# Loads, layer-norm roots, dummy matmuls and the job order of a one-core transformer kernel

## The chip, the core and the metric

The kernel runs on one core of a Trainium2 chip. The core has five engines that run their own instruction streams: PE (TensorE, matrix products, and transposes as products with an identity), DVE (VectorE), ACT (ScalarE), POOL (GpSimd) and SP (SyncE, here a queue that issues DMAs). They wait for each other on semaphores; each executes its own stream in order. Products accumulate in PSUM, which has 8 banks of 512 f32 columns; SBUF holds the rest. The metric is device time in microseconds of one execution, median of the runs.

## The reference

A layer norm of x (2048 tokens, width 448) feeds two branches, and the output is their sum with x:

```python
x = A_x
xn = _layernorm(x, axis=-1)
return x + _A_ref(xn, A_wqkv, A_w_phi, A_wo) + _B_ref(xn, B_w1, B_w2, B_w3, B_w4)

# A: 16 heads of 28; q, k, v from xn @ wqkv
pq = einsum("bhsd,hdf->bhsf", q, w_phi)          # the same for k
phi_q = concat([softmax(pq), softmax(-pq)])      # the same for k
kv = einsum("bhsf,bhsd->bhfd", phi_k, v);  z = einsum("bhsf->bhf", phi_k)
o = einsum("bhqf,bhfd->bhqd", phi_q, kv) / (einsum("bhqf,bhf->bhq", phi_q, z) + 1e-6)
A = o @ wo

# B: a mixer with four quarters of h shifted by 1, -1, 2, -2 tokens, then an MLP of width 1792
h = gelu(layernorm(xn) @ w1)
x1 = xn + shift(h) @ w2
B = x1 + gelu(layernorm(x1) @ w3) @ w4
```

## The kernel before

All inputs are bf16. The tokens are 16 tiles of 128 (t0 to t15), in 4 groups of 512. The width of 448 is split into 4 chunks of which PE works on row halves: a matmul uses either the lower or the upper 64 rows of the array, and one of each runs at a time. A product therefore has a list of lower and a list of upper matmuls, and writes its bank first from one half, then from the other.

A small recording layer (`Recorder`) takes the operations in the order in which the program text makes them, works out which semaphores each must wait for, and plays them to the engines. So the order of the text is the order of every engine's stream, of the two queues of DMAs (SP's, and ACT's, whose issues stand among ACT's work) and of PE above all.

The head (up to about 38 us in the profile):
- Loads: x tiles by `load_x`, wv and w1 by `load_half` in two halves (256 rows each, overlapping by 64), on SP and ACT by turns (L367 to L379). Then wphi, and `load_wT`: the q and k blocks of wqkv, transposed by DMA (t=1 for k, t=0 for q). `load_w2`, `load_w4` and `load_lap(w3)` come later, all on SP.
- Layer norm of a tile: "m" statistics and aggregate on DVE, "r" the power -0.5 on POOL (`ln_scale`), "a" the apply on DVE, or "p" the apply on POOL after a negated mean (`ln_neg`). The sums of tile 1 are made on ACT instead (`ln1_sums`).
- `XT`: the normalised tile transposed on PE into two banks (`xn_T`) and moved to `xnT` by ACT or DVE (`xn_out`); `XD`: the same by a DMA.
- `ZV(i)`: v of tile i into bank vb[i], moved by ACT or DVE (`EV`). `ZW(g, m)`: 128 columns of w1 for a group of 512 tokens into bank gb[g][m], gelu by ACT (`EW`). `ZR`: the last 64 columns of w1. `FO`: w_phi folded into a q or k block (`fold`), evicted by DVE. `rest_T` and `h_shift` are DMAs that bring h in place for w2.
- `HF`: halves of the first pair's products with the folded k and q and with w2.
- `spin` writes dummy matmuls on a constant to keep PE going; `busy`, their operand, is a piece of gT that DVE fills.

`chain` takes these jobs and lays the lower matmuls of a job out at once, its upper ones after a lag of 600 columns, between the lower ones of later jobs.

The rest is one list, played in order. For a pair n of tiles: (k0,n),(k1,n) and (q0,n),(q1,n) are first and second halves of the products, each followed by two Exp on ACT; (w0,i),(w1_,i) the w2 product and its sum into xn on DVE; kn and kx normalise phi_k (DVE, POOL); K is kv of a tile; T, G transposes by DMA; lo, sc, A the second layer norm; (a,p),(b,p) first and second half of a w3 product of 256 columns, followed by a gelu; N the attention output of a tile; (f,1..4,k) four parts of the last product for two tiles; S the store. The pair's banks are `kq[n]` and `wb[i]` (pair b means banks 2b and 2b+1).

Of the kernel before, what the change touches and what calls it, by code (L numbers as in the profile page):

```python
# [224 lines left out]
def bass_parallel_sum__linear_kernel_hedgehog__mixer_s_mlp__prompt_kernel(  # L225
# [17 lines left out]
    with es:  # L243
# [50 lines left out]
        wo = wv  # L294
# [116 lines left out]
        busy = gT[:, 0, 0, 0:256]  # L411
        R.ew(dve, "memset", busy, 1.0)
# [78 lines left out]
        def spin(n, cols):  # L491
            for _ in range(n):
                R.mm(banks[7][:, 0:cols], busy[:, 0:128], busy[:, 0:cols], True, True)
# [393 lines left out]
        def ln1(*ops):  # L887
            for op, *n in ops:
# [11 lines left out]
        fb = {(1, 0): 2, (1, 2): 2, (0, 0): 2, (0, 2): 5}  # L900
# [34 lines left out]
        kq = {0: (2, 0), 1: (1, 3), 2: (0, 1), 3: (0, 2), 4: (1, 2), 5: (1, 2), 6: (1, 2), 7: (1, 0)}  # L935
        wb = {0: 3, 2: 2, 4: 2, 6: 0, 8: 0, 10: 0, 12: 2, 14: 2}
# [3 lines left out]
        def HF(p, n):  # L940
# [4 lines left out]
        vb = {0: 7, 1: 6, 2: 0, 3: 2, 4: 4, 5: 5, 6: 1, 7: 0, 8: 4, 9: 5, 10: 0, 11: 6, 12: 3, 13: 2, 14: 0, 15: 1}  # L945
        gb = ((5, 2, 3), (7, 6, 5), (4, 1, 0), (7, 7, 4))
        spin(39, 128)
        ln1_sums(1)
        chain([
            L(("m", 0), ("m", 2), ("r", 0, 1), ("a", 0), ("m", 3), ("v", 1), ("r", 1, 2), ("a", 2), ("a", 1), ("r", 3, 1)),  # L950
            XT(0, 2, 1, "ACT"), do(spin, 5, 256), L(("a", 3), ("m", 4), ("m", 5), ("r", 4, 1), ("r", 5, 1)),
            inside(1, ZV(0, EV(0, "ACT", 1)), XT(2, 5, 1, "ACT")), XT(3, 3, 1, "ACT"), ZV(2, EV(2, "ACT", 1)),
            inside(1, ZV(3, EV(3, "ACT", 1)), XT(1, 3, 1, "ACT")), ZV(1, EV(1, "ACT", 1)), L(("a", 4), ("m", 7)),
            ZW(0, 0, EW(0, 0, 1)), L(("a", 5)), XT(5, 0, 1, "ACT"),
            L(("m", 6), ("m", 9), ("r", 7, 1), ("m", 8), ("r", 6, 1), ("r", 8, 1), ("a", 7), ("a", 6), ("m", 10)), ZW(0, 2),
            L(("m", 11), ("a", 8)), XD(8), L(("m", 12)), XT(4, 0, 1, "ACT"), L(("r", 9, 1)), ZW(0, 1, EW(0, 1, 2)), L(("a", 9)),
            ZV(4, EV(4, "ACT", 1)), XD(9), XT(7, 0, 1, "ACT"), L(("r", 10, 2), ("a", 10)), XT(6, 6, 1, "ACT"), L(("m", 13)),
            ZV(5, EV(5, "ACT", 1)), do(phi_blocks), ZV(7, EV(7, "DVE", 1)), ZW(1, 1, EW(1, 1, 1)), ZV(6, EV(6, "ACT", 1)),
            L(("p", 11), ("r", 12, 1), ("m", 15)), inside(2, ZW(1, 0, EW(1, 0, 1)), XT(10, 2, 1, "ACT")), L(("r", 13, 1)),
            ZW(1, 2, EW(1, 2, 1)), L(("p", 12), ("r", 15, 1)), inside(3, ZV(8, EV(8, "ACT", 1)), FO(1, 0, 0)), L(("m", 14)),  # L960
            XD(11), L(("r", 14, 1)), do(load_wT, 0, (1, 2, 3)), L(("a", 13)), inside(1, ZV(10, EV(10, "ACT", 1)), FO(1, 0, 1)),
            L(("a", 15)), ZR(0, 7, (rest_out, 0, 7), (rest_T, 0), (h_shift, 0)), ZV(9, EV(9, "DVE", 1)), XT(12, 3, 1, "ACT"),
            L(("p", 14)), do(load_w2), XT(13, 1, 1, "ACT"), ZV(11, EV(11, "ACT", 1)), ZW(2, 2, EW(2, 2, 1)), do(late_3),
            XT(14, 2, 2, "DVE"), ZW(2, 0, EW(2, 0, 1)), ZW(2, 1, EW(2, 1, 1)), do(load_lap, w3, B_w3), FO(1, 2, 0),
            inside(3, ZW(3, 0, EW(3, 0, 1)), FO(1, 2, 1)), ZR(1, 6, (rest_out, 1, 6)),
            inside(3, ZW(3, 2, EW(3, 2, 1)), FO(0, 0, 0)), ZV(15, EV(15, "ACT", 1)), do(kv_ones),
            inside(3, ZW(3, 1, EW(3, 1, 1)), FO(0, 0, 1)), do(rest_T, 1), inside(1, ZV(14, EV(14, "ACT", 1)), FO(0, 2, 0)),
            FO(0, 2, 1), ZV(13, EV(13, "ACT", 1)), ZV(12, EV(12, "DVE", 1)), HF(0, 0), do(kv_picks), HF(1, 0), HF(2, 0), HF(0, 1),
            do(h_shift, 1), HF(1, 1), do(load_w4), HF(2, 1)], 600, 1)

        on_dve = (4, 6, 7, 9, 12)
# [58 lines left out]
        def wo_in():  # L1030
            load_lap(wo, A_wo)
# [3 lines left out]
            (T, 0), (T, 1), (k0, 1), (w0, 2), (kn, 0), (k1, 1), (w1_, 2), (lo, 0), (q0, 1), (k0, 2), (kx, 0), (k1, 2), (kn, 1), (w0, 4),  # L1035
            (kx, 1), (q1, 1), (T, 2), (T, 3), (q0, 2), (lo, 1), (w1_, 4), (kn, 2), (q1, 2), (T, 4), (T, 5), (lo, 3), (k0, 3), (K, 0), (k1, 3), (kn, 3),
            (kx, 2), (lo, 2), (kx, 3), (q0, 3), (sc, 0), (K, 1), (q1, 3), (T, 6), (T, 7), (A, 1), (A, 0), (k0, 4), (G, 0), (A, 3), (w0, 6),
            (A, 2), (K, 2), (k1, 4), (G, 1), (G, 2), (K, 3), (G, 3), (q0, 4), (w1_, 6), (q1, 4), (k0, 5), (K, 4), (kn, 4),
            (w0, 8), (k1, 5), (q0, 5), (kx, 4), (K, 5), (lo, 4), (w1_, 8), (kn, 5), (q1, 5), (K, 6), (k0, 6), (w0, 10),
# [49 lines left out]
```

## Time and profile before

| | us |
|---|---|
| median of 3 runs (173.91 to 174.32) | 173.97 |
| the profiled execution | 174.06 |
| its span, first to last instruction | 172.3 |

The granted clock of TensorE is 1.00 in every stretch of the span. By stretch, busy time in us of each engine (and its instructions), as the profile's windows give it:

| stretch, us | what runs | PE | DVE | ACT | POOL |
|---|---|---|---|---|---|
| 0 to 7.57 | loads, dummies, first tiles' layer norm | 5.12 (x53) | 3.93 (x13) | 3.51 (x7) | 4.22 (x23) |
| 7.57 to 15 | v, w1, layer norm | 7.20 (x109) | 7.19 (x21) | 5.46 (x11) | 3.54 (x6) |
| 15 to 33 | v, w1, folds | 17.96 (x359) | 11.66 (x30) | 13.40 (x24) | 9.03 (x15) |
| 33 to 46 | first pairs | 12.90 (x135) | 9.69 (x17) | 10.56 (x13) | 3.87 (x2) |
| 46 to 80 | k, q, w2, kv, first w3 | 33.97 (x564) | 29.29 (x45) | 26.05 (x31) | 28.12 (x16) |
| 80 to 88 | w3, first attention tiles | 7.91 (x104) | 7.27 (x21) | 3.35 (x5) | 3.69 (x5) |
| 88 to 165 | w3, w4, attention out | 77.00 (x958) | 40.43 (x107) | 19.68 (x20) | 36.90 (x56) |
| 165 to 172.3 | last tiles, stores | 4.84 (x44) | 1.41 (x3) | 0.00 (x0) | 0.65 (x1) |

Busy time of PE is the union of pipelined matmuls, so a stretch can look full while single matmuls start late. ACT loads a function table three times: at 0.80 (gelu), 34.18 (Exp) and 67.41 (gelu), 1.28 each. The first transfers, from issue to landing: x0 and x1 2.4 and 2.6, x2 and x3 2.6 and 2.8, the wv halves 4.8 (SP) and 5.7 (ACT), x4 and x5 5.4 and 5.8, the w1 halves 6.2 and 6.5; a half of w3 4.8 and 6.5, w4 10.0.

### The profile page before, as it was taken

What the parts mean: (1) busy time and instruction counts of PE and PEld (TensorE: products, weight loads), DVE (VectorE), ACT (ScalarE), POOL (GpSimd) and SP (SyncE); (2) the same over time, 40 slices, a digit from 0 to 9 for tenths busy, and PEclk for the clock granted to TensorE, in tenths of its full rate; (3) what the DMA queues carried; (4) which work ended last, traced back from release to release, by engine and by line L of the source; (5) the groups of instructions that cost most, each with busy time, mean ns of one, the idle gap of its engine ahead of it and who ended that gap; (6) DMA issues with size and microseconds to landing.
All of it is one profiled execution on the core that took longest, in us unless ns stands there. A gap on an engine that the chain in (4) does not pass through costs nothing.

```text
span 172.3 us, 5315 instructions
## 1 busy us (share of the span) xinstructions
PE 166.9 (97%) x2308; PEld 96.6 (56%) x2308; DVE 110.9 (64%) x251; ACT 82.0 (48%) x107; POOL 90.0 (52%) x121
## 2 busy tenths in 40 slices
PE   7799999999999999999999999999999999999994
PEld 7545888874555555554544554554545545555563
DVE  3799943749999989918955873525817416474621
ACT  4478876777987899646133322133133212044000
POOL 5456970004779999860574289332441522724540
PEclk9999999999999999999999999999999999999999
DMA  5995546499998955161057557554961120233331
GB/s 127 330 248 92 104 67 158 87 352 220 334 159 174 135 124 138 21 76 30 11 114 97 111 105 146 94 103 106 136 135 34 30 57 4 57 34 84 88 87 50
DMA packets 51111, 20.07 MB, mean 116 GB/s; under 512 B 42256, under 2 KB 50384, under 8 KB 51088
## 3 DMA queue, kind: packets, MB, share of 16 engines
q1 hardware_dynamic: 49968, 18.86, 56.0%
q10 hardware_dynamic: 1120, 0.87, 1.6%
q8 instruction: 18, 0.29, 0.8%
q14 instruction: 5, 0.04, 0.1%
HBM read 7.14 MB, written 1.84 MB: 52 GB/s over the span
## 4 chain that ended last, share of the span: by engine, by line
PE 92%; DMA 3%; ACT 1%; DVE 1%; issue 0%; ACTq 0%
PE banks L204 91%; DMA wv<-in_A_wqkv_dram 3%; PE banks L208 1%; ACT xnT L212 1%; DVE wpq L216 1%; ACT vaug L212 0%; ACTq L222 0%; ACT L366 0%; DVE vaug L216 0%
## 5 line engine op out<-in xcount | busy, mean ns | idle before, releaser
L212 ACT ACTIVATE phik<-banks 128x1024 bf16<-128x1024 f32 (+1 forms) x44 | 42.2, 986 | 63.6 <-PE banks L204 63.4
L204 PE MATMUL banks<-gT,w 64*128 64x512 bf16 x392 | 49.2, 376 | 0.1
L216 DVE TENSOR_TENSOR vaug<-banks,vaug 128x464 f32<-128x464 f32 (+3 forms) x65 | 32.8, 513 | 20.6 <-PE banks L204 18.9
L204 PE MATMUL banks<-w,phik 64*128 64x448 bf16 (+3 forms) x434 | 45.2, 343 | 0.0
L216 POOL TENSOR_TENSOR xnT<-vaug 128x196 bf16<-128x196 f32 (+1 forms) x32 | 18.1, 587 | 47.8 <-DVE vaug L216 47.8
L204 PE MATMUL banks<-wv,xnT 64*128 64x448 bf16 (+3 forms) x222 | 32.8, 346 | 1.4 <-DMA wv<-in_A_wqkv_dram 1.2
L204 PEld LDWEIGHTS banks<-w,phik 64*128 64x128 bf16 (+1 forms) x434 | 22.9, 94 | 19.4 <-issue 0.4
L722 POOL TENSOR_TENSOR phik<-phik,rks 128x1792 bf16<-128x1792 bf16 x8 | 25.6, 3214 | 10.7 <-DVE rks L216 10.5
L204 PEld LDWEIGHTS banks<-gT,w 64*128 64x128 bf16 x392 | 18.0, 94 | 18.7 <-PE banks L204 1.1
L204 PEld LDWEIGHTS banks<-wv,xnT 64*128 64x128 bf16 (+1 forms) x222 | 13.8, 94 | 10.0 <-ACT xnT L212 1.6
L216 POOL TENSOR_TENSOR vaug<-xn,xtok 128x448 f32<-128x448 bf16 x16 | 16.2, 1033 | 0.2 <-DVE vaug L216 0.2
L216 DVE TENSOR_REDUCE ksum<-phik 128x64 f32<-128x1792 bf16 x8 | 16.0, 1994 | 0.0
L216 POOL TENSOR_TENSOR rs<-mv,mhalf 128x1 f32<-128x1 f32 (+2 forms) x18 | 12.4, 694 | 6.6 <-DVE mv L216 6.6
L204 PE MATMUL banks<-xnT,w 64*128 64x512 bf16 x84 | 15.7, 377 | 0.0
L216 DVE RECIPROCAL vaug<-banks 128x16 f32<-128x16 f32 x16 | 4.0, 252 | 17.4 <-PE banks L204 17.4
L204 PE MATMUL banks<-wpk,xnT 64*128 64x448 bf16 x112 | 14.9, 350 | 0.1
L212 ACT ACTIVATE hi<-banks 128x896 bf16<-128x896 f32 x16 | 13.8, 931 | 1.0 <-PE banks L204 1.0
L204 PE MATMUL banks<-wpq,xnT 64*128 64x448 bf16 x112 | 14.2, 349 | 0.0
L204 PE MATMUL banks<-w,hT 64*128 64x448 bf16 x96 | 12.9, 349 | 0.0
L216 DVE TENSOR_TENSOR xn<-banks,xn 128x512 bf16<-128x512 f32 (+1 forms) x16 | 9.0, 606 | 3.0 <-PE banks L204 2.9
L216 DVE BATCH_NORM_STATS2 st<-xn 128x6 f32<-128x448 bf16 x16 | 9.4, 589 | 0.0
L216 DVE BATCH_NORM_STATS2 st<-xtok 128x6 f32<-128x448 bf16 x15 | 9.1, 606 | 0.0
(72 smaller groups left out, 165.4 us busy)
## 6 DMA issues: line engine op xcount, KB each, us to landing
w<-in_B_w_dram SPq DMA_DIRECT2D x2, 896.0 KB, 5.7
out_dram<-vaug SPq DMA_DIRECT2D x15, 112.0 KB, 2.0
w<-in_B_w_dram SPq DMA_DIRECT2D x1, 1568.0 KB, 10.0
xtok<-in_A_x_dram SPq DMA_DIRECT2D x2, 448.0 KB, 7.4
wv<-in_A_wo_dram SPq DMA_DIRECT2D x2, 224.0 KB, 2.9
xtok<-in_A_x_dram SPq DMA_DIRECT2D x3, 112.0 KB, 2.6
xtok<-in_A_x_dram ACTq DMA_DIRECT2D x3, 112.0 KB, 2.8
w<-in_B_w_dram SPq DMA_DIRECT2D x1, 336.0 KB, 4.3
```

The costliest lines, as they stand in the source:

```text
L204: self.op("PE", lambda e: e.matmul(out, lhsT, rhs, start=start, stop=stop, skip_group_check=True), [out], [lhsT, rhs], tile=self._tile(lhsT))
L208: self.op("PE", lambda e: e.transpose(out, in_, ident), [out], [in_, ident], tile=self._tile(in_))
L212: self.op("ACT", lambda e: e.activation(out, in_, func, **kw), [out], [in_] + aps)
L216: self.op(eng, lambda e: getattr(e, name)(out, *args, **kw), [out], aps)
L722: R.op(pool, lambda e: e.tensor_tensor(ph, ph, wide, op=ALU.mult), [ph], [ph, wide, *after])
```

## The change

- wv's halves are issued right after x0 and x1, ahead of x2 and x3; half 0 of wv and of w1 is now SP's, half 1 ACT's.
- The roots of tiles 1 to 7 are made on ACT ("q", `ln_root`), whose preloaded table is now that of the reciprocal root; a table load before the first gelu is added by that.
- Tiles 2, 3, 4, 5, 7, 12, 14, 9, 10, 11 are applied on POOL (before: 11, 12, 14), the others on DVE. Tiles 9 to 12 go through DMA transposes (before: 8, 9, 11).
- The first group of w1 is made in halves of 256 tokens (`ZH`), three products of two halves each. `z_h`, which nothing called, is removed.
- The dummies read a constant tensor; besides `spin`, `HD` puts short groups of half-height dummies between the first tiles.
- w2 is loaded on ACT's queue, w3 in two halves at two places (the second behind w4 and the h shifts), wo on ACT's queue.
- Banks vb, gb, fb, kq, wb are given anew, and both lists are in another order.

```diff
-        R.op("ACT", lambda e: e.preload_act_table_set("gelu_apprx_tanh_and_others"), [], [])
+        R.op("ACT", lambda e: e.preload_act_table_set("abs_reciprocal_sqrt_and_small"), [], [])
         load_x(0, 1)
         load_x(1, 1, "ACT")
+        load_half(wv, wv_d, 0)
+        load_half(wv, wv_d, 1, "ACT")
         load_x(2, 1)
         load_x(3, 1, "ACT")
-        load_half(wv, wv_d, 1)
-        load_half(wv, wv_d, 0, "ACT")
         load_x(4, 1)
         load_x(5, 1, "ACT")
-        load_half(w1, B_w1, 1)
-        load_half(w1, B_w1, 0, "ACT")
+        load_half(w1, B_w1, 0)
+        load_half(w1, B_w1, 1, "ACT")
...
-        busy = gT[:, 0, 0, 0:256]
-        R.ew(dve, "memset", busy, 1.0)
+        busy = nc.const_aps.tensor(1.0, [128, 128], BF16)
...
+        def ln_root(a, n):
+            R.act(rs[:, a:a + n, 0], mv[:, a:a + n, 1], ACT.Abs_reciprocal_sqrt)
...
-        def spin(n, cols):
+        def spin(n):
             for _ in range(n):
-                R.mm(banks[7][:, 0:cols], busy[:, 0:128], busy[:, 0:cols], True, True)
+                R.mm(banks[7][:, 0:128], busy, busy, True, True)
+
+        def hold(b, n):
+            return [[(banks[b + k][:, 0:128], busy[r, :], busy[r, :], True) for _ in range(n)]
+                    for k, r in enumerate((slice(0, 64), slice(64, 128)))]
...
+                if eng == "2":
+                    R.act(d[:, :, 0, :], a[:, :, 0, :], ACT.Copy)
+                    R.ew(dve, "tensor_copy", d[:, :, 1, :], a[:, :, 1, :])
...
+        def z_w1h(m, b, h):
+            c = slice(256 * h, 256 * h + 256)
+
+            def make(rows, kcs):
+                lo, hi = rows
+                return [(banks[b][:, c], w1[lo:hi, kc, 128 * m:128 * m + 128], xnT[lo:hi, kc, c],
+                         rows == LO and n == 0 and h == 0) for n, kc in enumerate(kcs)]
             return make
...
-        kq = {0: (2, 0), 1: (1, 3), 2: (0, 1), 3: (0, 2), 4: (1, 2), 5: (1, 2), 6: (1, 2), 7: (1, 0)}
-        wb = {0: 3, 2: 2, 4: 2, 6: 0, 8: 0, 10: 0, 12: 2, 14: 2}
+        kq = {0: (3, 2), 1: (3, 3), 2: (0, 1), 3: (0, 3), 4: (1, 2), 5: (1, 2), 6: (1, 2), 7: (1, 0)}
+        wb = {0: 0, 2: 1, 4: 2, 6: 0, 8: 0, 10: 0, 12: 2, 14: 2}
...
-        spin(39, 128)
+        spin(30)
         ln1_sums(1)
         chain([
-            L(("m", 0), ("m", 2), ("r", 0, 1), ("a", 0), ("m", 3), ("v", 1), ("r", 1, 2), ("a", 2), ("a", 1), ("r", 3, 1)),
-            XT(0, 2, 1, "ACT"), do(spin, 5, 256), L(("a", 3), ("m", 4), ("m", 5), ("r", 4, 1), ("r", 5, 1)),
-            inside(1, ZV(0, EV(0, "ACT", 1)), XT(2, 5, 1, "ACT")), XT(3, 3, 1, "ACT"), ZV(2, EV(2, "ACT", 1)),
...
+            do(spin, 3), L(("m", 0), ("r", 0, 1), ("a", 0), ("v", 1), ("m", 2)), L(("q", 1, 1)), do(spin, 3), HD(2, 3),
+            L(("a", 1)), HD(0, 3), L(("m", 5)), XT(0, 4, 1, "ACT"), L(("q", 2, 1)), HD(2, 3), HD(2, 3), L(("p", 2)),
+            HD(6, 2), XT(1, 2, 1, "ACT"), L(("m", 3)), ZV(0, EV(0, "ACT", 1)), L(("q", 5, 1)),
+            inside(1, ZH(2, 0), XT(2, 6, 1, "ACT")), L(("p", 5), ("m", 4), ("q", 3, 1), ("m", 6)), ZV(1, EV(1, "ACT", 1)),
+            L(("m", 7), ("q", 4, 1)), inside(1, ZV(2, EV(2, "ACT", 1)), XT(5, 6, 1, "ACT")), L(("p", 3)), L(("q", 6, 1)),
+            ZH(1, 0), XT(3, 4, 1, "2"), ZV(5, EV(5, "ACT", 1)), L(("q", 7, 1), ("a", 6), ("m", 12)), ZH(0, 0), L(("p", 4)),
+            ZH(0, 1, EW(0, 0, 1)), XT(4, 4, 1, "ACT"), XT(6, 0, 1, "DVE"), ZH(2, 1), L(("p", 7)), ZH(1, 1, EW(0, 1, 2)),
+            L(("r", 12, 1)), XT(7, 4, 1, "ACT"), L(("m", 14)), ZV(3, EV(3, "ACT", 1)), ZV(4, EV(4, "ACT", 1)),
+            ZW(1, 0, EW(1, 0, 1)), L(("p", 12)), L(("m", 15), ("r", 14, 1)), XD(12), do(load_w3, 0),
+            L(("r", 15, 1), ("p", 14), ("m", 13), ("r", 13, 1), ("m", 10), ("a", 15), ("r", 10, 1)),
+            do(load_wT, 0, (1, 2, 3)), ZW(1, 1, EW(1, 1, 1)), ZV(6, EV(6, "ACT", 1)), L(("m", 9)), XT(14, 2, 2, "DVE"),
...
         play([
-            (T, 0), (T, 1), (k0, 1), (w0, 2), (kn, 0), (k1, 1), (w1_, 2), (lo, 0), (q0, 1), (k0, 2), (kx, 0), (k1, 2), (kn, 1), (w0, 4),
...
-            (kc,), (w1_, 14), (b, 5), (kb,), (a, 6), (b, 6), (lo, 8), (N, 0), (T, 8), (a, 7), (lo, 11), (lo, 10), (f, 1, 0), (N, 1), (T, 9),
-            (b, 7), (a, 8), (sc, 8), (A, 10), (A, 8), (b, 8), (f, 2, 0), (lo, 12), (A, 9), (G, 8), (A, 11), (G, 9), (a, 9),
...
+            (w0, 2), (k0, 1), (kn, 0), (w1_, 2), (T, 0), (k1, 1), (k0, 2), (w0, 4), (kn, 1), (k1, 2), (T, 1), (q0, 1),
+            (lo, 0), (kx, 0), (q0, 2), (q1, 1), (w1_, 4), (q1, 2), (k0, 3), (q0, 3), (T, 2), (kx, 1), (k1, 3), (kn, 2),
...
+            (a, 5), (wo_in, "ACT"), (a, 6), (sc, 8), (kb,), (b, 5), (A, 9), (b, 6), (N, 0), (f, 1, 0), (N, 1), (a, 7),
+            (a, 8), (A, 8), (A, 10), (T, 11), (b, 7), (b, 8), (f, 2, 0), (lo, 13), (A, 11), (G, 10), (a, 9), (lo, 12),
...
```

## The prediction, made before the changed kernel was run

> **What bounds the kernel now.** I read the busy shares, then the chain of waits, then the timeline of PE. The shares say that PE is the bound of the whole span:
>
> ```profile
> span 172.3 us, 5315 instructions
> PE 166.9 (97%) x2308; PEld 96.6 (56%) x2308; DVE 110.9 (64%) x251; ACT 82.0 (48%) x107; POOL 90.0 (52%) x121
> ```
>
> The chain of waits (start, length, what) shows where PE is not the bound: until wv has landed, in two places of the head where ACT moves a transposed tile (10.08, 12.39), and at the last folded weight (30.18).
>
> ```profile
> 1.74 5.70 DMA wv<-in_A_wqkv_dram
> 7.43 0.14 issue
> 7.57 0.21 PE banks L204
> ...
> 10.08 0.50 ACT xnT L212
> ...
> 12.39 0.61 ACT xnT L212
> ...
> 30.18 1.10 DVE wpq L216
> ...
> 169.88 0.36 DVE vaug L216
> ```
>
> The timeline of PE gives its pace and its hidden stalls (start, length, what, count):
>
> ```profile
> 13.17 1.03 PE L204 MATMUL banks<-xnT,w 64*128 64x512 bf16 x8
> 40.33 0.92 PE L204 MATMUL banks<-wpq,xnT 64*128 64x448 bf16 x8
> 41.09 1.73 PE L204 MATMUL banks<-wpk,xnT 64*128 64x448 bf16 x14
> 78.93 1.92 PE L204 MATMUL banks<-gT,w 64*128 64x512 bf16 x14
> 84.81 2.57 PE L204 MATMUL banks<-gT,w 64*128 64x512 bf16 x20
> ```
>
> Matmuls run in pairs, one per row half. One of 512 columns lasts 0.38, so four pairs in 1.03 start (1.03-0.38)/3 = 0.217 apart; with 448 columns, (0.92-0.35)/3 = 0.190. That is 2.4 columns per ns plus 2.5 ns a matmul. By that pace the other three rows should last 6x0.19+0.35 = 1.49, 6x0.217+0.38 = 1.68 and 9x0.217+0.38 = 2.33: each is 0.24 too long. In each, the second half of a job follows the first half at once ((k0,2) and (k1,2); (a,6) and (b,6); (a,8) and (b,8)) and writes the same banks from the other row half, which waits for PE's own last writes.
>
> I gave every matmul of the order of before this pace, summed per row half and took the longer half: 159.46 us from the first wv matmul on. 7.57 + 159.46 = 167.03, but PE's last matmuls stand at 169.68. So 2.65 us after 7.57 are stalls, and only these, the start, and the work itself can change: 0.85 from 8 to 15, about 0.7 from 28 to 39, 0.7 in the three self-waits, and 0.4 in small ones.
>
> **The change, part by part.**
>
> *Work.* Twelve PE transposes of tiles instead of thirteen, the products of w1's rest in another balance of row halves, and tile 1's transposes ahead of the first wv matmul: the same sum is 159.11 for the order of after, -0.35. Halving the first w1 chunk streams the same columns (21+21 of 256 for 21 of 512). The dummies (36 full, 28 half ones) fill time in which PE has nothing; the 39 of before went 0.107 apart until 5.07, so 48 from about 0.85 end at 5.3, before tile 0 is normalised (5.37).
>
> *Start.* wv is second on both queues. Landings of before by place in the queue: SP 3.2, 3.9, then wv 1.71+4.8 = 6.5, x4 7.6, w1 8.9; ACT 3.4, 4.1, then wv 7.4, x5 8.0, w1 9.2. In both kernels 448 KB stand up to the third place, so x2 should land at 6.5 and wv before it, between the second and third place (4.1 to 7.4; I take 5.8 and 6.8). But DVE now has the statistics of x2 ahead of tile 1's apply, and PE has tile 1's transposes ahead of the first wv matmul. Statistics 6.57 (landing +0.1), aggregate 7.30, apply 7.41 to 7.82, transposes 7.87 to 8.01: the first wv matmul goes from 7.57 to 8.01, +0.44, and wv is not what it waits for. If x2 lands at 4.1 this is 6.9, but then the first w1 half (8.9) holds the third job anyway, so the gain is at most 0.3; if at 7.4, it costs 0.9 more.
>
> *Head to 18 us.* Tiles 2 to 5, 7, 12 and 14 are applied on POOL, tiles 2 to 7 with the root on ACT. Rows:
>
> ```profile
> 18.49 0.19 POOL L216 TENSOR_SCALAR rs<-mv 128x1 f32<-128x1 f32 x1
> 18.77 0.77 POOL L216 TENSOR_SCALAR xn<-xtok,rs 128x512 bf16<-128x512 bf16 x1
> ...
> 21.13 0.77 POOL L216 TENSOR_SCALAR xn<-xtok,rs 128x512 bf16<-128x512 bf16 x1
> ```
>
> So a tile on POOL costs 0.29+0.77 = 1.06 (0.41 on DVE before). A root on ACT shows nowhere; bounds are the 0.20 of the one-column ACT row at 4.21 and the 0.56 of POOL's power; I take 0.20, the same engine and shape. Walking the queues with these, 0.49 from one ACT move to the next and 0.84 for statistics and aggregate on DVE:
> - w1's first half lands 8.86, its matmul starts 8.98 where PE is free at 8.76: 0.2.
> - x5 (8.06): aggregate till 9.09, root 9.34, POOL 9.42 to 10.48; PE wants it at 10.44: 0.1. Tile 3 follows on POOL till 11.50, wanted 11.47: 0.1.
> - Tile 6's transposes need the bank of v2, which ACT empties 12.85 to 13.39 because the root of tile 7 stands ahead; wanted 13.17: 0.25.
> - A new table load before the first gelu: 15.28 to 16.56, gelus till 18.1. Tiles 14 and 15 need those banks; PE arrives at 18.05: 0.1, the rest is hidden behind five jobs whose banks are free. Without that cover it would cost 1.28.
>
> With small gaps at switches, 1.0 is lost from 8.01 to 20, where before lost 0.85 by 25.
>
> *20 to 37 us.* Tile 8's apply stands on DVE behind the eviction of a folded weight (1.09, from about 22.0), so its transposes come 0.3 late. On SP, half of w3 (896 KB) goes ahead of the three last transposed wq blocks: before, such a half took 4.8 to land and the transposes 2.9 to 3.8; issued after tile 12's transpose (17.1), they land by 24.1 to 26, and PE wants the last at about 25.1: 0 to 0.9, I take 0.2. w2's three issues on ACT (about 0.46 each, as the wv row at 1.74) end before its next gelu is needed. The first hRT transpose is queued behind six h shifts (0.6 each) and lands near 34.5, wanted at 35.5. I add 0.2 for the rest; before lost 0.7 here.
>
> *37 us to the end.* Every first and second half now has other work between. That removes the three self-waits (0.7); the other 0.4 may be replaced: I leave 0.2. I checked each w3 job against the gelu that frees its banks (1.02+0.2): the least cover is 1.40. On SP, w4 goes out some 6 us earlier (about 33 for 39.3; it took 10.0), the second h shifts and half of w3 (4.8) behind it, then the transposes of q: the first should land near 47 (50.2 before), wanted by the fifth pair's Exp at 53.6; the shifts near 44, wanted at 51. wo's issue on ACT lies in idle time (3.75 before one gelu).
>
> *Sum.* 8.01+159.11 = 167.12; +1.0+0.7+0.2 = 169.0 against 169.68: -0.7. The profiled execution took 174.06 with a span of 172.3; the median of the runs is 173.97. 173.97-0.7 = **173.3 us**.
>
> *A rule against this change.* Before, the last Exp, the load and the first gelu stand so:
>
> ```profile
> 65.66 1.73 ACT L212 ACTIVATE hi<-banks 128x896 bf16<-128x896 f32 x2
> 67.41 1.28 ACT L212 ACT_TABLE_LOAD   x1
> 68.70 1.02 ACT L212 ACTIVATE phik<-banks 128x1024 bf16<-128x1024 f32 x1
> ```
>
> The gelu starts 0.01 after the load, the load 0.02 after the Exp: a switch costs 1.3. The Trainium skill (ScalarE: Activation LUTs, "What ACT_TABLE_LOAD costs") puts 1.28 for the load and another 1.38 of drain on every switch; this trace shows no such drain.
>
> **The rivals.**
> 1. *The head runs clean* (tile and root shorter, x2 early): its 1.0 shrinks to 0.3 and the start to 7.7. 173.3-0.7-0.1 = 172.5. For: PE's waits in my walk are 0.1 each, near the error of a row. Against: tile 6 and w1 are fixed by rows.
> 2. *Nothing is left*: the re-ordered jobs make as many self-waits and bank waits as they remove, so the 0.7 of the end doesn't come: 174.0. For: six of the jobs' bank pairs changed. Against: in the written order no two halves are neighbours.
> 3. *Slower: POOL bounds the head.* From 9.4 to 18 POOL has six tiles and three powers in series, and each is fed by an ACT root behind a DVE aggregate behind x5's landing. Its tile took 0.91 at 16.57 and its power up to 0.68: six times 0.14 and three times 0.1 make tile 14 late by 1.1, of which 0.3 is slack; x5 0.5 later (its bounds are x4's 7.6 and w1's 9.2) adds 0.5. 173.3+1.3 = 174.6. It decides once tile 14 ends after 18.1, and is slower than before once it ends after 18.8. For: POOL is idle there now, DVE has slack it no longer needs. Against: two of three rows are 0.77.
> 4. *Slower: w3's half holds the wq blocks*: the last lands at 26.5, +1.2: 174.5.
> 5. *Slower: a drain behind the new table load.* If ACT stood idle after it as long as after the load at 34.18 (1.18, there put down to PE), the gelus would end at 19.3 and tiles 14 and 15 wait that long: 173.3+1.2 = 174.5. For: no load stands amid crowded ACT work in this trace. Against: the row at 68.70. The Trainium skill's page on ScalarE, above, is the rule for it; by its 1.38 the estimate would be 174.7.
>
> **How the numbers follow.** Forecast 0.45 (own range 172.8 to 173.9), rival 1 0.17, rival 2 0.13, rival 3 0.14, rival 4 0.05, rival 5 0.06. A difference under 0.3%, 0.5 us, can't be told from none: faster is below 173.45, slower above 174.5. Of the forecast's 0.45 some 0.31 lie below 173.45. Faster 0.31+0.17 = 0.48; same 0.14+0.13 = 0.27; slower 0.25. The range is 172.3 to 174.7: it takes in rivals 1 to 4 and the bounds of x2 and of the blocks.
>
> **What would show it.** The first wv matmul near 8.0, right after tile 1's transposes, with DVE's statistics of x2 ahead; an ACT table load near 15.3 and tiles 14 and 15 close behind the gelus; no wait over 0.2 on PE after 37. I am wrong if the first wv matmul starts before 7.4 or after 8.6, if PE waits for a wq block or for POOL more than 0.5, or if waits of PE on itself are still there after 40.

## The result and the profile after

| | before | after |
|---|---|---|
| median, us (6 runs each, side by side) | 174.03 (173.79 to 174.32) | 176.06 (175.60 to 177.85) |
| ratio to before, 95% interval | | 1.0127 [1.0098, 1.0157] |
| measured again beside other kernels | 174.35 (17 runs) | 177.06 (6 runs), 1.0144 [1.0091, 1.0196] |
| profiled execution and its span | 174.06, 172.3 | 176.22, 174.5 |

The change makes the kernel slower by 2.0 us. 173.3 was predicted, with a range up to 174.7. Intervals here leave executions that were disturbed out; medians and ranges are of all.

The page of the changed kernel, first its busy shares:

```profile
span 174.5 us, 5399 instructions
PE 166.2 (95%) x2341; PEld 101.4 (58%) x2341; DVE 112.4 (64%) x247; ACT 81.7 (47%) x112; POOL 92.2 (53%) x129
```

PE's busy time is 0.7 us less (166.9 before); the span has grown by 2.2, so PE waits more. The waits (in total, times, longest) say for what; PEld is PE's load of weights:

```profile
POOL phik L734 <- DVE g_tok L216: 3.3, 1, 3.3
PEld banks L204 <- POOL phik L734: 2.0, 1, 2.0
...
PE banks L204 <- DMA xnT<-xn: 1.7, 1, 1.7
PEld banks L204 <- DMA hi<-in_A_wqkv_dram: 1.2, 3, 0.4
```

Three places, none of which was on the prediction's list of PE's waits as large as this: the q blocks of wqkv (1.2), one tile that a DMA transposes (1.7), and POOL's product of phi_k (2.0). In the timeline of PE (start, length, what, count, idle time before and its releaser) they stand here:

```profile
24.05 0.21 PE L204 MATMUL banks<-g_tok,hi 48*128 48x56 bf16 x2 [0.25 <-DMA hi<-in_A_wqkv_dram]
24.54 0.21 PE L204 MATMUL banks<-g_tok,hi 48*128 48x56 bf16 x2 [0.27 <-DMA hi<-in_A_wqkv_dram]
...
27.93 0.35 PE L204 MATMUL banks<-wv,xnT 64*128 64x448 bf16 x1 [1.65 <-DMA xnT<-xn]
...
79.62 0.63 PE L204 MATMUL banks<-vaug,phik 64*128 64x59 bf16 x32 [1.90 <-POOL phik L734]
```

To see what each is worth I used the prediction's pace: the start of a matmul plus all work that is left behind it is the end that PE would reach without a further stall, its projected end. A wait costs 0.1 to 0.3 more in this end than the idle time that the timeline gives. Both kernels by time:

| near, us | before | after | after minus before |
|---|---|---|---|
| first wv matmul (7.57; 6.71) | 167.0 | 165.8 | -1.2 |
| 22 | 167.85 | 166.40 | -1.45 |
| 28 | 168.09 | 169.76 | +1.7 |
| 77 | 169.1 | 169.91 | +0.8 |
| 81 | 169.5 | 171.97 | +2.45 |
| end | 169.68 | 171.90 | +2.2 |

So the head gains 1.45 until 22 us. Between 22 and 28 this and 1.7 more is lost for two DMA waits. From 28 to 77 the kernel before loses 1.0 in its self-waits and small stalls and the changed one 0.15, so 0.9 comes back. One wait at 79.6 costs 2.05.

SP's queue around the first two (start, length, what, count):

```profile
14.21 1.26 SPq L219 DMA_TRANSPOSE xnT<-xn  x1
15.52 1.78 SPq L222 DMA_DIRECT2D w<-in_B_w_dram  x1
17.35 3.74 SPq L219 DMA_TRANSPOSE hi<-in_A_wqkv_dram  x3
21.13 5.63 SPq L219 DMA_TRANSPOSE xnT<-xn  x3
```

The second row is the half of w3 (896 KB), the third the q blocks, the fourth tiles 10, 11 and 9. w3 lands at 21.63, the q blocks at 23.54, 24.01 and 24.49, tile 10 at 27.79. On ACT's queue the three parts of w2 are issued from 21.00 on and land at 25.61, 27.53 and 28.16.

The third wait, in the timelines of DVE and POOL of the changed kernel (kn6 and kn7 are the sums of phi_k for the last two pairs, kx6 and kx7 POOL's products for them):

```profile
70.02 3.51 DVE L216 TENSOR_SCALAR g_tok<-xn,mv,rs 128x512 bf16<-128x512 bf16 x2
73.45 2.00 DVE L216 TENSOR_REDUCE ksum<-phik 128x64 f32<-128x1792 bf16 x1
75.49 0.55 DVE L216 RECIPROCAL rks<-ksum 128x64 f32<-128x64 f32 x1
75.96 0.32 DVE L216 TENSOR_SCALAR g_tok<-xn,mv,rs 128x512 bf16<-128x512 bf16 x1
...
69.84 3.21 POOL L734 TENSOR_TENSOR phik<-phik,rks 128x1792 bf16<-128x1792 bf16 x1
76.36 3.21 POOL L734 TENSOR_TENSOR phik<-phik,rks 128x1792 bf16<-128x1792 bf16 x1 [3.30 <-DVE g_tok L216]
```

Two applies (A6, A7) take 3.51 us. One by one, A6 takes 3.18 and ends 0.14 after POOL's kx6 (69.84 to 73.05), as if kx6 had held it; A7, behind it, takes 0.40. In the kernel before, three of the same shape took 1.36:

```profile
67.58 1.98 DVE L216 TENSOR_REDUCE ksum<-phik 128x64 f32<-128x1792 bf16 x1
71.23 1.36 DVE L216 TENSOR_SCALAR g_tok<-xn,mv,rs 128x512 bf16<-128x512 bf16 x3
...
71.42 1.03 POOL L216 TENSOR_SCALAR g_tok<-xn,rs 128x512 bf16<-128x512 bf16 x1 [0.22 <-POOL rs L216]
72.68 3.21 POOL L722 TENSOR_TENSOR phik<-phik,rks 128x1792 bf16<-128x1792 bf16 x1 [0.23 <-DVE g_tok L216]
```

Even here the third apply took 0.71 beside POOL's apply (71.42 to 72.45) and ended 0.15 after it. The first two took 0.41 each, though the second also began behind POOL's start, and POOL's own took 1.03 where others of its shape take 0.77: either side can be the one that is delayed. In the changed kernel the sums kn7 stand behind A6 and A7, the apply A4 behind kn7, and kx7, POOL's last product of phi_k, waits for A4; the kv products of tiles 14 and 15 wait for kx7. Before, kn7 started at 67.58 and kx7 ended at 75.89, and the same products waited for nothing.

### The profile page after: what moved, and what is told of

Same layout as the page of the kernel before. It is cut to its first block, busy times and chain, and to the rows that moved or that the text cites. A ratio compares the mean times of both kernels' runs of the same rounds, so it can differ in the third digit from the quotient of the medians.

```text
span 174.5 us, 5399 instructions
## 1 busy us (share of the span) xinstructions
PE 166.2 (95%) x2341; PEld 101.4 (58%) x2341; DVE 112.4 (64%) x247; ACT 81.7 (47%) x112; POOL 92.2 (53%) x129
## 4 chain that ended last, share of the span: by engine, by line
PE 73%; POOL 9%; DVE 9%; DMA 5%; issue 1%; ACT 0%; DVEq 0%
PE banks L204 73%; DMA xnT<-xn 4%; POOL rs L216 4%; POOL xn L216 4%; DVE ksum L216 2%; DVE g_tok L216 2%; DVE st L216 2%; POOL phik L734 2%; DVE xn L216 2%; DMA xtok<-in_A_x_dram 1%; DVE mv L216 1%; ACT xnT L212 0%; DVE rks L216 0%; DVE vaug L216 0%; PE banks L208 0%
## 5 line engine op out<-in xcount | busy, mean ns | idle before, releaser
L212 ACT ACTIVATE phik<-banks 128x1024 bf16<-128x1024 f32 (+1 forms) x44 | 41.5, 985 | 60.0 <-PE banks L204 59.9
L204 PE MATMUL banks<-gT,w 64*128 64x512 bf16 x392 | 48.3, 376 | 0.0
L204 PE MATMUL banks<-wv,xnT 64*128 64x448 bf16 (+3 forms) x222 | 34.5, 346 | 1.7 <-DMA xnT<-xn 1.7
L204 PEld LDWEIGHTS banks<-w,phik 64*128 64x128 bf16 (+1 forms) x434 | 24.3, 94 | 17.9 <-issue 0.4
L204 PEld LDWEIGHTS banks<-gT,w 64*128 64x128 bf16 x392 | 19.3, 94 | 17.3 <-ACT phik L212 0.6
L204 PEld LDWEIGHTS banks<-wv,xnT 64*128 64x128 bf16 (+1 forms) x222 | 14.9, 94 | 8.3 <-DVE wpq L216 1.9
L204 PE MATMUL banks<-xnT,w 64*128 64x512 bf16 (+1 forms) x105 | 18.5, 333 | 0.1
L216 POOL TENSOR_TENSOR rs<-mv,mhalf 128x1 f32<-128x1 f32 (+1 forms) x13 | 8.9, 697 | 1.7 <-DVE mv L216 1.7
L212 ACT ACTIVATE hT<-banks 128x512 bf16<-128x512 f32 (+1 forms) x11 | 6.8, 643 | 6.3 <-PE banks L204 6.2
L204 PEld LDWEIGHTS banks<-xnT,w 64*128 64x128 bf16 x105 | 8.0, 94 | 2.7 <-ACT xnT L212 0.5
```

Source lines behind the costliest of these rows:

```text
L204: self.op("PE", lambda e: e.matmul(out, lhsT, rhs, start=start, stop=stop, skip_group_check=True), [out], [lhsT, rhs], tile=self._tile(lhsT))
L212: self.op("ACT", lambda e: e.activation(out, in_, func, **kw), [out], [in_] + aps)
L216: self.op(eng, lambda e: getattr(e, name)(out, *args, **kw), [out], aps)
```

## Experiments: the transfers of the head

Theory: half of w3 ahead of the q blocks and w2 beside tile 10 make the two DMA waits. All five runs are the changed kernel with issues moved in the list.

**w3 just behind the q blocks.**

```diff
-XD(12), do(load_w3, 0),
+XD(12),
...
-do(load_wT, 0, (1, 2, 3)), ZW(1, 1, EW(1, 1, 1)),
+do(load_wT, 0, (1, 2, 3)), do(load_w3, 0), ZW(1, 1, EW(1, 1, 1)),
```

> Half 0 of w3 is issued just behind the three q blocks of wqkv instead of ahead of them; it still stands ahead of tile 10's DMA transpose. If the queue order is why PE waits 0.30, 0.43 and 0.44 us for the q blocks (landings 23.54, 24.01, 24.49), these land about 2.5 us earlier, near 21 to 22, and the three waits go. If tile 10 (landing 27.79) is held by w2 and w3, it lands no earlier, PE waits some 1.2 longer there instead (2.8 in place of 1.65), and the time stays at 176.0 (175.6 to 176.4). Rival: tile 10's transpose is late because it is queued behind the q blocks themselves; then it lands with them 2.5 earlier and the time is 173.0.

(A half of w3 is 896 KB, not the 448 of these texts.) Measured 179.89 (178.36 to 180.82), ratio to before 1.0298 [1.0208, 1.0387]. The q blocks land at 20.18 to 22.59 and their waits are gone, so queue order made them. But w3, issued at 21.09, and w2 now stand right ahead of tile 10, which lands at 30.13, 8.4 us after its issue. PE waits 4.65 for it, and its clock falls. The windows of this run (PE busy comes first, PEclk is the third number from the end):

```profile
26.00:28.00 2.00, 0.00 (x0) 0.00 (x0) 0.66 (x1) 0.00 (x0) 0.00 (x0) 1.00 1.26 243
28.00:30.00 2.00, 0.00 (x0) 0.00 (x0) 0.00 (x0) 0.00 (x0) 0.00 (x0) 0.57 1.66 74
30.00:32.00 2.00, 1.74 (x24) 1.51 (x25) 0.00 (x0) 0.34 (x1) 0.00 (x0) 0.50 1.21 206
32.00:34.00 2.00, 2.00 (x43) 1.83 (x41) 1.09 (x1) 0.80 (x2) 0.00 (x0) 0.50 0.20 30
34.00:36.00 2.00, 2.00 (x39) 1.67 (x37) 0.00 (x0) 0.82 (x2) 0.00 (x0) 0.72 0.03 8
```

After the wait PE works at half its clock for some 5 us. The expectation had the place of the new wait right, its size (2.8) too small and so the time (176.0), and knew nothing of the clock.

**w3 behind the last tile's transpose:**

```diff
-XD(12), do(load_w3, 0),
+XD(12),
...
-XD(9),
+XD(9), do(load_w3, 0),
```

> Half 0 of w3 is issued behind the last DMA transpose of a tile (tile 9), so neither the q blocks nor tiles 10, 11 and 9 have it ahead of them; w2 stays. If w2 alone holds tile 10, the q blocks' waits go but tile 10 lands at about 26 to 27.8 and the gain is 0 to 1.4 us (174.6 to 176.0). If w3's 448 KB is what delays everything behind it, tile 10 lands near 24 and both waits go: 176.0-1.2-1.7 = 173.1. If transfers later in the head (h shifts, w4, DMA share 0.98 from 32 to 46) are the real limit, PE waits there instead, for h or w2, and less than 1 us is won.

174.61 (173.50 to 177.11), 1.0006 [0.9964, 1.0048]. The q blocks do not wait. Tile 10 is issued at 20.80, before w2 (21.26 to 22.28), yet lands at 27.07, between w2's parts (26.63, 27.27, 27.68); PE waits 1.95. So w2 holds it alone, although on another queue and issued later. The profiled execution is the slowest of the ten (177.11): its clock falls to 0.50 from 28.39 to 31.80, behind that wait, which adds 1.6 to the projected end.

**w2 later**, w3 as in the changed kernel:

```diff
-do(load_w2, "ACT"), XT(8, 5, 1, "DVE"),
+XT(8, 5, 1, "DVE"),
...
-ZV(8, EV(8, "ACT", 1)), FO(0, 2, 1),
+ZV(8, EV(8, "ACT", 1)), do(load_w2, "ACT"), FO(0, 2, 1),
```

> w2's three issues stand on ACT some five jobs later (near 26 instead of 21); w3 stays ahead of the q blocks. If w2's transfers hold tile 10's transpose, it lands at 25.5 to 26.3 and its wait of 1.65 goes, the q blocks' waits stay: 176.0-1.7 = 174.3 (174.0 to 174.8). If tile 10 is held by what is ahead of it on its own queue, it lands at 27.8 as before: 176.0. If w2 is then late for its first product (near 38), a new wait appears there and eats up to 1 us.

175.82 (173.38 to 178.88), 1.0019 [0.9966, 1.0073]. Tile 10 lands at 26.51 and PE waits 0.65 for it; the q blocks hold PE as before. So w3 in front of it makes it late too (the next run has neither), and the wait does not go as expected. In the profiled execution the clock falls to 0.50 behind the wait for kx7 (79.6 to 83.0 us), which adds 1.7 to the projected end. The longest executions have a mean clock of 0.98 to 0.99 and the shortest of 1.00, so the spread comes from such falls, and the median says less than the landings do.

**Both later** (the edits of the last two runs):

> Both: half 0 of w3 behind tile 9's transpose and w2 some five jobs later. If the waits of the head add and nothing behind them absorbs the gain, 176.0-1.4-1.8 = 172.8 (172.4 to 173.4), with PE's projected end 3.2 us earlier from 29 us on and the wait for the last product of phi_k (1.9) unchanged. Rival: from 32 to 46 the DMA engines are 0.98 busy, and from 46 to 80 DVE is 0.97 busy, so what the head wins is lost again there as waits for h, w2 or the norms: 174 to 175.

176.78 (175.58 to 179.80), 1.0105 [1.0009, 1.0202]. Tile 10 lands at 23.21, 3.0 after its issue, and neither it nor the q blocks make PE wait: the two causes are right. The gain is lost again, though: w3, issued at 25.70 just ahead of the first h shifts, lands at 34.28 and the shifts at 34.5 to 36.9, and PE waits 2.85 at 37.16 for the transpose of h right behind them, which w2's product needs. This is the rival, though the time lies above its 174 to 175; w3 has only been moved in front of the next transfer that PE needs. The profiled execution is the slowest of the four (179.80): its clock falls to 0.50 twice, at 37.40 and at 81.77, for 3.41 us each.

**w3 at the end of the head**, w2 as above:

```diff
-XD(12), do(load_w3, 0),
+XD(12),
...
-do(h_shift, 1), do(load_w3, 1),
+do(h_shift, 1), do(load_w3, 0), do(load_w3, 1),
```

> Half 0 of w3 stands behind the second h shifts, right ahead of its other half, so that nothing but what PE waits for is on SP in the head; w2 as in the run with both later. The q blocks land near 20 to 22.7, tile 10 near 23.2, and the first h shifts, now without w3 ahead of them, by 34: no wait of PE over 0.3 from 8 to 45, projected end 3.2 us ahead of the changed kernel's from 29 on, kx7's wait of 2.06 unchanged: 176.0-3.2 = 172.8 (172.3 to 173.4; up to 1.7 more where the clock falls behind kx7's wait). Rival: the head's gain is lost to the q transposes, which now stand behind 896 KB more on SP: 174 or more, with a PE wait after 45.

174.71 (173.49 to 176.42), 1.0023 [0.9995, 1.0052]. From 9 to 45 us one wait is left, which costs 0.65 (tile 9 behind w2, at 29.78), the projected end at 75 is 168.7 (changed kernel: 169.9) and kx7's wait still costs 2.1; the clock did not fall behind it in this execution. Expected were 172.8; in this execution the first half of w1 landed at 8.79 (7.54 in the changed kernel's first profile) and its product waited 1.1. The q transposes, behind 1792 KB, hold nothing up.

## Experiments: the last product of phi_k

**kn7 ahead of A6 and A7.**

```diff
-(A, 6), (A, 7), (kn, 7), (A, 4),
+(kn, 7), (A, 6), (A, 7), (A, 4),
```

> DVE's sums of phi_k's last pair (kn7) stand ahead of the applies A6 and A7, not behind them; nothing else is moved. Theory: kx7 starts late because kn7 stands behind A6 and A7, which last 3.51 us instead of about 0.6 as POOL's kx6 runs. Then kn7 ends near 72.6, A6, A7 and A4 follow when kx6 ends (73.05), kx7 runs 73.9 to 77.1, and the wait of the kv products (1.9) goes: 176.0-2.0 = 174.0 (173.6 to 174.4). Rival: the four statistics ahead of kn6 alone make it late; then kx7 comes no more than 0.5 us earlier: 175.5.

175.03 (172.53 to 176.30), 0.9982 [0.9945, 1.0019]. kx7 runs from 74.68 to 77.9 and PE does not wait for it, as the theory said. The time is 1.0 above the 174.0 expected. In the profiled execution (175.74) the head was 1.1 later by 22 us, with w1's first half landing at 8.65, and half of the gain is given back at 85.95, where a w3 product waits 0.73 (a cost of 0.9) for a transposed tile of the second layer norm.

**POOL made to wait.** This tells order from overlap: DVE's order stays, kx6 gets a wait for A6 and A7 (`g_tok` slots 2 and 3).

```diff
-k_product(2 * n, [g_tok[:, :, :]] if n == 7 else [])
+k_product(2 * n, [g_tok[:, :, :]] if n == 7 else [g_tok[:, 2, :], g_tok[:, 3, :]] if n == 6 else [])
```

> DVE's order is that of the changed kernel, kn7 behind A6 and A7; only POOL's product kx6 is given a wait for A6 and A7, so that they do not overlap. If the overlap with a POOL instruction is what stretches A6 and A7, they take 0.6 (70.0 to 70.6), kn7 ends at 73.1, A4 is done by about 74.1 behind kx6 (70.6 to 73.8) and kx7 runs 74.1 to 77.3: the added wait makes the kernel 2.0 us faster, 174.0. Rival: A6 and A7 are slow for another reason (their own input late); then the wait delays kx6 to 73.6 and kx7 to 76.8 or later: 176.0 to 176.8.

175.25 (174.76 to 176.98), 1.0084 [1.0048, 1.0119]. DVE and POOL of this run:

```profile
70.66 0.73 DVE L216 TENSOR_SCALAR g_tok<-xn,mv,rs 128x512 bf16<-128x512 bf16 x2
71.31 2.01 DVE L216 TENSOR_REDUCE ksum<-phik 128x64 f32<-128x1792 bf16 x1
...
73.82 1.01 DVE L216 TENSOR_SCALAR g_tok<-xn,mv,rs 128x512 bf16<-128x512 bf16 x1
...
71.48 3.21 POOL L734 TENSOR_TENSOR phik<-phik,rks 128x1792 bf16<-128x1792 bf16 x1 [0.93 <-DVE g_tok L216]
74.92 3.21 POOL L734 TENSOR_TENSOR phik<-phik,rks 128x1792 bf16<-128x1792 bf16 x1 [0.23 <-DVE g_tok L216]
```

With kx6 held back by 0.93 the two applies last 0.73 instead of 3.51, and kx7 starts 1.4 us earlier, in an execution whose DVE was 0.6 later when A6 began. PE's matmuls do not wait for kx7. The sum kn7 runs beside kx6 in its usual 2.0; the apply A4, which meets kx6's end (74.69), takes 1.01 instead of 0.32 and again ends 0.14 after it. So an apply of this shape that starts beside POOL's product of phi_k ends only with it in these runs, and a reduction is not held. This is the rule of the Trainium skill (SBUF — State Buffer, "Who interferes with whom"): DVE's fast two-port form of `tensor_scalar` and a GpSimd instruction share a port pair that the first holds for its whole length, while `tensor_reduce` never needs it. By the rule the loss would be kx6's remaining 3.0, an estimate; the trace has 3.51 - 0.73 = 2.8. The time won is less than the 2.0 expected: the head of this profiled execution ran 0.65 later than the first profile's by 22 us, which the experiment did not touch.

## Experiments: all together

**All mended**: the edits of w3_last_w2_later and of kn7_first.

> The last run's loads and kn7 ahead of A6 and A7. If the three waits are all that the new orders cost, they add: 176.0-3.2-2.0 = 170.8 (170.3 to 171.4), faster than both kernels, at a clock of 1.00 throughout as PE has no wait over 1 us. Rival: with the head 3 us earlier DVE, 0.97 busy from 46 to 80, becomes what PE waits for: 171.5 to 172.8.

172.72 (172.52 to 174.00), 0.9915 [0.9894, 0.9935]. Faster than both kernels, but 1.9 short of the sum. Its profiled execution (174.00, the slowest of the six) shows two new waits that cost 1.2 each: tile 9 at 29.70, behind w2, and a first w3 product at 67.16, whose last transposed tile was issued at 62.56 and landed at 66.92. The view of waits puts the second down to an Exp of ACT, but in queues_in_order_again the same product starts at 64.63, amid that Exp (64.03 to 65.76). Nor is it the order of the queue: the q transposes had landed by 60.60, nothing else was under way, and the same transpose took 2.48 in w3_last_w2_later, which has the same transfers, against 4.36 here. It is one slow landing, whose cause stays open.

**Queues in order**: w2 two jobs later still than in all_mended, and w4 out of the head into the list behind the first four g transposes.

```diff
-ZV(8, EV(8, "ACT", 1)), do(load_w2, "ACT"), FO(0, 2, 1),
+ZV(8, EV(8, "ACT", 1)), FO(0, 2, 1),
-inside(1, ZV(10, EV(10, "ACT", 1)), FO(0, 0, 0)), FO(0, 0, 1),
+inside(1, ZV(10, EV(10, "ACT", 1)), FO(0, 0, 0)), do(load_w2, "ACT"), FO(0, 0, 1),
...
-do(load_w4), HF(2, 0),
+HF(2, 0),
...
-(G, 0), (K, 8),
+(G, 0), (load_w4,), (K, 8),
```

> all_mended with two more transfers out of the way: w2 two jobs later still, behind tile 9's transpose, and w4 (needed by the last product only, near 82) behind the first four transposes of the second layer norm. The run all_mended still had waits of 1.16 (tile 9's transpose, landing 29.65 behind w2) and 1.20 (a transpose of the second layer norm, issued 62.56 behind q transposes, landing 66.92). If the order of the queues makes both, they go: 172.7-2.3 = 170.4 (170.0 to 171.2). Rival: the DMA engines as a whole are the limit, so another transfer (w2 near 36, or the q transposes) is late instead: 171.5 to 173.

172.63 (171.62 to 175.29), 0.9879 [0.9844, 0.9914], and once more:

> queues_in_order once more, as the yardstick on this chip: 172.4 (171.6 to 172.8) where the clock stays at 1.00; executions with a fall of the clock up to 2.5 us longer.

171.88 (171.45 to 172.60), 0.9867 [0.9835, 0.9900]: 2.3 us faster than before; the first of the two runs is 4.4 faster than the changed kernel beside it. Tile 9 now lands at 27.13 (first run) and PE does not wait for it. The 170.4 expected is not reached (shortest execution 171.45), and what w4's new place is worth is not shown, as no order made the wait at 67.16. All that is left of the waits of PE's matmuls, in the second run's view of waits (the first line is the start of the program):

```profile
PE banks L204 <- PEq L1097: 0.8, 1, 0.8
PE banks L204 <- ACT vaug L212: 0.2, 1, 0.2
```

The changed orders therefore hold a kernel that is faster than the one before; the waits for the q blocks, tile 10 and kx7 hid it. The changed kernel itself, beside these:

> The changed kernel itself, beside the others on one chip, to measure them against. 176.0 (175.5 to 176.5), with PE's waits for the q blocks (1.2 in all), for tile 10 (1.7) and for phi_k's last product (1.9 to 2.1), as in its first profile; executions in which the clock falls behind one of these waits are up to 2 us longer.

177.06 (175.79 to 178.18). In its profiled execution (178.18) tile 10 holds PE 1.92 and the clock falls to 0.50 behind it, which takes 1.8 more by the projected end; behind kx7's wait of 1.93 the clock stays at 1.00.

## Experiments: the parts of the head

**wv first, alone, on the kernel before.**

```diff
-load_x(2, 1)
-load_x(3, 1, "ACT")
 load_half(wv, wv_d, 1)
 load_half(wv, wv_d, 0, "ACT")
+load_x(2, 1)
+load_x(3, 1, "ACT")
```

> The kernel before with one part of the change alone: both halves of wv issued ahead of x2 and x3. If the earlier wv is what won the head's 1.0 to 1.5 us, the first wv matmul goes from 7.57 to about 6.9 and the time to 173.3. Rival, and what I expect: there tile 0's apply stands on DVE behind the statistics of x2, which now lands later (near 5.3 for 4.3), so the start is won and lost again: first wv matmul 7.4 to 8.0, time 173.7 to 174.4.

177.29 (176.30 to 178.09), 1.0169 [1.0126, 1.0213]. The order that I expected to be worth nothing costs 3 us. PE of this run:

```profile
4.75 0.72 PE L204 MATMUL banks<-gT 128*128 128x128 bf16 x6
6.97 0.29 PE L208 MATMUL banks<-ident,xn 64*128 64x64 bf16 x8 [1.50 <-DVE xn L216]
7.20 0.72 PE L204 MATMUL banks<-gT 128*128 128x256 bf16 x5
7.96 0.36 PE L204 MATMUL banks<-wv,xnT 64*128 64x448 bf16 x1
9.04 0.39 PE L208 MATMUL banks<-ident,xn 64*128 64x64 bf16 x8 [0.72 <-DVE xn L216]
9.25 0.93 PE L204 MATMUL banks<-wv,xnT 64*128 64x448 bf16 x2
```

x2 lands at 5.75 (3.86 before), and tile 0's apply stands behind its statistics (6.54 for 4.96): that was expected, and wv at 5.2 is of no use. Two idle stretches of 1.5 and 0.7 follow, and from 8.6 to 15.4 us the clock is 0.50; by 17 us the projected end has gone from 166.9 to 171.7. So wv first does not pay with the old order of the norms. In the changed kernel, whose new order puts tile 0 ahead of x2, the first wv matmul starts 0.86 earlier than before; that the new order makes the difference was not tested alone.

**Roots back on POOL**, in queues_in_order, which also takes the second table load away:

```diff
-R.op("ACT", lambda e: e.preload_act_table_set("abs_reciprocal_sqrt_and_small"), [], [])
+R.op("ACT", lambda e: e.preload_act_table_set("gelu_apprx_tanh_and_others"), [], [])
...
-                    ln_root(*n)
+                    ln_scale(mv, rs, *n)
```

> queues_in_order with the roots of tiles 1 to 7 back on POOL and the gelu table preloaded, so no second table load. POOL is 0.92 busy from 10 to 20; seven powers of 0.4 to 0.56 more are 3 to 4 us on it, of which DVE's and ACT's lead hides part: tiles 3, 4, 7, 12 and 14 come late and PE waits 1 to 3 us more in the head than in queues_in_order, at most 1.3 of it given back by the table load. Expected: 1 to 2.5 us slower than queues_in_order. Rival: the table load (1.28 at 13.5) and ACT's seven roots cost as much as they win: within 0.4 of it.

174.44 (173.89 to 176.72), 1.0018 [0.9987, 1.0048]; queues_in_order beside it 172.63. The medians differ by 1.8 us, the two ratios to before by 2.4. Two waits show 1.4 of it, both for tiles that POOL applies:

```profile
12.35 0.29 PE L208 MATMUL banks<-ident,xn 64*128 64x64 bf16 x8 [0.96 <-POOL xn L216]
14.43 0.41 PE L208 MATMUL banks<-ident,xn 64*128 64x64 bf16 x16 [0.46 <-POOL xn L216]
```

**Without the short dummies**, in queues_in_order:

```diff
-do(spin, 3), HD(2, 3),
-L(("a", 1)), HD(0, 3), L(("m", 5)), XT(0, 4, 1, "ACT"), L(("q", 2, 1)), HD(2, 3), HD(2, 3), L(("p", 2)),
-HD(6, 2), XT(1, 2, 1, "ACT"),
+do(spin, 3),
+L(("a", 1)), L(("m", 5)), XT(0, 4, 1, "ACT"), L(("q", 2, 1)), L(("p", 2)),
+XT(1, 2, 1, "ACT"),
```

> queues_in_order without the 28 half-height dummies between the first tiles. If they keep the clock up, PE, which then has next to nothing from 4.4 to 8 but two tiles' transposes and four products, falls to half clock near 7 to 9 for some 3.4 us, as behind the longer waits of the other runs: 1.5 to 2 us slower than queues_in_order. Rival: PE's waits there are set by x1 and w1 anyway and the window is too short to count: within 0.3 of it.

173.84 (171.49 to 174.88), 0.9888 [0.9823, 0.9952], against 171.88. One of four executions is as fast as with them, so the size is not settled. In the profiled one (174.36) PE waits 1.4 for tile 1 at 6.98, and a 448-column matmul lasts 0.55 to 0.58 until 13 us, where it is 0.35 elsewhere. It lasts as long (0.55 to 0.58) in before_wv_first from 9.2 to 14.8 us, where the clock on record is 0.50, so this is half clock. The expectation had it fall near 7 to 9; here it had not risen yet. PE's transposes at 5.1, ahead of the wait, already take 0.23 to 0.24, and 0.19 from 13 us on. In the changed kernel a 128-column dummy takes 0.31 up to 4.0 us and 0.22 from 4.4 on, so there the clock rises before the first tile. (The windows give 1.00 for such a start, because the trace's record of the clock begins with the rise: at 13.19 here, at 4.29 in the changed kernel, and at 5.11 in the kernel before, whose first dummies take 0.31 as well. The 1.00 given for every stretch of its span holds from there on.) By 13.4 the projected end is 3.0 worse.

**w1's first group whole**, in queues_in_order:

```diff
-inside(1, ZH(2, 0), XT(2, 6, 1, "ACT")),
+XT(2, 6, 1, "ACT"),
...
-ZH(1, 0), XT(3, 4, 1, "2"),
+XT(3, 4, 1, "2"),
...
-ZH(0, 0), L(("p", 4)), ZH(0, 1, EW(0, 0, 1)),
+L(("p", 4)), ZW(0, 0, EW(0, 0, 1)),
...
-ZH(2, 1), L(("p", 7)), ZH(1, 1, EW(0, 1, 2)),
+ZW(0, 2), L(("p", 7)), ZW(0, 1, EW(0, 1, 2)),
```

> queues_in_order with the first w1 group in whole products of 512 tokens, at the places of the second halves. Between 7 and 12 us PE then has only v of tiles 0, 1, 2 and 5 and their transposes: 4 x 0.78 of products in a stretch where a tile comes every 1.1 us, so some 1.2 us more of waiting, and less cover for the layer norm: 1.0 to 1.5 us slower, up to 3 if the clock falls. Rival: w1 lands at 8.0 to 8.6, so its first half-products wait for it (0.6 to 1.3 us in every run); without them this wait is gone and the halves are worth nothing: within 0.4.

173.30 (173.02 to 174.33), 0.9949 [0.9925, 0.9972], against 171.88: the halves are worth 1.4, in waits of 0.2 to 0.6 from 7 to 16.

## Why the prediction was wrong, step by step

- *What bounds the kernel* and *work*: right. PE's pace held, and its busy time went from 166.9 to 166.2.
- *Start*: wrong by 1.3. The first wv matmul came at 6.71, right behind tile 1's transposes as said, not at 8.01; x2 landed at 5.32, where I took 6.5 out of bounds of 4.1 and 7.4. The landing was read off the third place of the one profile before, on the ground that the same 448 KB stand up to it. In all 16 profiles with wv second, x2 in third place landed at 5.25 to 6.12; wv, which took 4.8 and 5.7 us before, took 3.2 to 4.4. Why the third place is earlier with wv in front is open.
- *Head*: 0.6 lost instead of 1.0. The root took 0.20 and POOL's tile 1.06 as priced. The table load ran from 13.46 to 14.74, 1.8 earlier than said:

```profile
12.84 0.60 ACT L212 ACTIVATE xnT<-banks 128x512 bf16<-128x512 bf16 x1
13.46 1.28 ACT L212 ACT_TABLE_LOAD   x1
14.75 1.51 ACT L212 ACTIVATE hT<-banks 128x512 bf16<-128x512 f32 x2
```

The gelu follows at once, so the drain of rival 5 is not there, and no tile waited for POOL as in rival 3. That the head runs clean (rival 1) is what happened, and more of it: PE was 1.45 ahead of before at 22. (Rival 1's sum takes 0.1 for a start of 7.7 in place of 8.01; it should be 0.3, and its time 172.3.)
- *20 to 37* is the first step that cost time. It failed in the words "they land by 24.1 to 26, and PE wants the last at about 25.1: 0 to 0.9, I take 0.2". They landed at 23.5 to 24.5, no later than said; but PE wanted the last near 23.4 (it started at 24.54 after 1.17 of waits), because the head was earlier. An earlier engine does not move a transfer that a queue holds. Rival 4 had this place and this price with a chance of 0.05, though by a later landing (26.5) that did not come.
- The same step wrote of w2 that its issues "end before its next gelu is needed". That priced ACT's 0.46 per issue, not the 448 KB, which from ACT's queue, together with w3 in front on SP's, held tile 10's transpose until 27.79: it lands at 27.07 without w3 in front, at 26.51 with w2 later, at 23.21 with both changes. No step gave tiles 9 to 12 a landing. Cost: 1.8.
- *37 to the end*: the self-waits did go (PE's loads waited 1.6 for PE in three places before, and the changed kernel's list has no such line), the gelu cover of the w3 products held, w4 and the shifts came in time. But "the other 0.4 may be replaced: I leave 0.2" left out the kv products, whose last wait cost 2.05 in place of 0.2. I had checked what frees PE's banks and not what feeds its operands, and priced POOL's and DVE's instructions as if they ran side by side.
- *Sum*: against 169.0, the start and head were 1.7 better, the DMA step 2.7 worse, the end 1.9 worse: 171.9.

## What to carry to other kernels

When work moves, list every transfer and every cross-engine chain that feeds the bounding engine with its landing and its wanted time, and take the wanted time at the earliest that the new head allows: gains upstream turn into waits at the first thing that did not move. Order transfers by when they are needed, over all queues together; a large one issued from another engine delays the small one beside it. And before one engine's long instruction is placed beside another's, look for a row in which both ran at once: the profile before had one, the third apply's 0.71 beside POOL's 1.03.

## What was not expected of the hardware

- The clock falls behind waits of PE of some 2 us, but not each time: of the twelve idle times of 1.65 to 1.95 in these profiles four were followed by a clock of 0.50, and so were both longer ones (2.85 and 4.65). Behind 1.90 for kx7 it fell in w2_later, and stayed at 1.00 behind 1.93 in changed_again, where it had fallen behind tile 10's 1.92. Five falls lasted 3.41 us and began 0.2 to 1.4 us after PE had started again; those measured cost 1.6 to 1.8. Two lasted 6.83 (w3_behind_wq, before_wv_first). The Trainium skill (TensorE: Matmul & The Clock Gate, "Why this matters for your kernels") warns of gaps over about 3 us; here 1.9 was enough.
- Without the short dummies the clock rose at 13.19 us in the profiled execution, with them by 6.7 in every profile, but there too at times that differ from one execution to the next (4.29 and 5.75 for the changed kernel).
- The same transfers land at other times from one execution to the next: w1's first half between 7.54 and 8.79 in the changed order, which moves the head by up to 1.2.
- A small DMA transpose took 2.5 to 3.0 us to land with nothing beside it (once 4.4, in all_mended) and up to 8.4 with 1344 KB in front and beside, although part of that was on another queue and issued after it. The Trainium skill (DMA: Bandwidth & Descriptors, "Issuing engines are not separate DMA queues") says that both queues run on the same 16 engines; the landings agree.
- DVE's apply beside a POOL product: 0.32 to 0.41 alone, 3.18 for the one that met kx6 near its start, while a reduction took 2.0 either way.
